# An attention and MLP kernel on one core: score slots handed over bank by bank, operands made earlier, fill products at the start, and a root by Ln and Exp

## The chip, the core and the metric

One Trainium2 chip, one of its cores. The metric is device microseconds from start to end of one execution; the median of three runs of the kernel before is 671.86 us (670.94 to 672.25). The core's engines run side by side, each in the order of its own program: TensorE (PE) for matrix products, VectorE (DVE) and GpSimd (POOL) for arithmetic on tiles, ScalarE (ACT) for functions and copies, and SyncE (SP), which issues most of the DMA transfers.

## The reference

Rotary attention over 4 batches, 8 heads, 576 positions and 64 channels per head; its result, as (batch, position, 512 channels), goes through a layer norm and a two-layer MLP with 2048 hidden channels and is added to it.

```
q_rot, k_rot = rotate(q), rotate(k)
scores = (q_rot @ k_rot^T) / sqrt(D)
attn = exp(scores - max(scores)); attn = attn / (sum(attn) + 1e-09)
x = concat over heads of attn @ v
mu, var = mean(x), mean((x - mu) ** 2)
xn = (x - mu) / sqrt(var + 1e-06) * g_ln
out = x + relu(xn @ w_ch1) @ w_ch2
```

All tensors are float32. The MLP's products are made of a high and a low part of each operand: three products (high weight by high and by low input, low weight by high input) stand for one.

## The kernel before

**Plan.** The kernel is first written down as tasks (`add`), each with an engine, the tasks it waits for and the buffers (`RINGS`, `LATE`) it takes and gives back. Two tables of digits, `PLACES` and `SIDES`, fix the order of the tasks and, for those that may run on DVE or on POOL, the engine. `Plan.run` goes through the tasks in that order and emits their instructions; every engine then works through its own in that order.

**Attention.** 16 pairs of heads, each in blocks of 128 queries. `scores` (L486, and L499 for the 64 queries left over) makes a block of scores in PSUM, in one of four "sc" banks of two halves; DVE finds the row maximum (L513), ACT the exponential with its sum (L520); transposes by identity products on PE (L580) or by DVE (L568) and copies (L598) follow; then pv (L654, L680) and the scaling into the row blocks xt (L692, L701, L706). Between these stand the decoding of the MLP's weights (L868 to L897) and, from the norm of block 0 on, that block's MLP in plain form (`mlp_unit`, L1007, its hidden values L1030 and L1034 and its sums L1044).

**Startup.** `warm` (L1310) multiplies the identity by itself 16 times on PE; `first_pair` loads keys, queries and the rotary table, and rotates them (L387): the first half of the keys, the query head (128 columns) and the second half of the keys on DVE, the remaining 448 queries on POOL. The memsets L361 to L364 stand between these.

**Layer norm.** For each of five row blocks: sums over channels (L759), mean by a product (L766), centring (L790), squares (L796), variance (L780), the root by ACT's Sqrt (L808) and DVE's reciprocal (L811), a spread of it over the partitions on PE (L816) and the scaling (L825). Block 0 goes to the plain MLP; blocks 1 to 4 are stored as "hats" (L838).

**Paired layers.** Blocks (1, 2) and then (3, 4), 448 columns each, go through the MLP in pairs with seven products in place of eight (`pair_stage`, L1180; the order of the products is 1, 6, 2, 7, 5, 4, 3). `pair_inputs` reloads the hats (L1126) and makes seven operands from differences of them (L1110), for two row groups: ACT rounds the high part (L1088), DVE or POOL makes the low part (L1095). A stage has two halves of six matmuls for each product; its PSUM slots "n", six halves, are read by DVE or ACT (L1221 to L1236 in a hidden stage, L1252 and L1276 in an output stage). The weights w come by DMA, 512 KB a product, some of them as sums made by L961 and L971. `switch` closes the attention's buffers and opens those of the paired layers, the "n" slots among them.

## Time and profile before

| | |
|---|---|
| median of 3 runs | 671.86 us (670.94 to 672.25) |
| profiled execution: its own time | 673.72 us |
| its span, from the first to the last instruction | 671.8 us |
| busy: PE, DVE, ACT, POOL | 630.5, 552.2, 358.5, 297.6 us |
| mean granted clock of PE | 0.987 of full speed |

The profile is of one execution. An engine's busy time is the time in which at least one of its instructions runs; idle time before an instruction is put down to what ended last before it began.

### The profile page before, as it was taken

The page shows a single profiled execution, that of the slowest core. Times are in us where ns is not written, and L with a number is a line of the kernel's source. Part 1 is how long each engine was busy: PE and PEld are TensorE (multiplying, and loading weights), DVE is VectorE, ACT ScalarE, POOL GpSimd, SP SyncE. Part 2 cuts the span into 40 slices and gives each one's busy share as a digit, 9 for nine tenths or more (in the row PEclk, how much of TensorE's full clock was granted, in tenths as well). Part 3 has the DMA queues.
Part 4 walks back from the last instruction along what each step waited for, and adds up shares of the span by engine and source line. Part 5 has one row for each costly group of instructions (what it writes and reads, how often), then busy time and mean ns, then how long its engine had stood idle before and what let it go on. Part 6 is the DMA issues. An engine that isn't in the chain of part 4 may idle for free.

```text
span 671.8 us, 13940 instructions
## 1 busy us (share of the span) xinstructions
PE 630.5 (94%) x5268; PEld 491.4 (73%) x5268; DVE 552.2 (82%) x887; ACT 358.5 (53%) x734; POOL 297.6 (44%) x223
## 2 busy tenths in 40 slices
PE   5899988999899999898898699899999999999997
PEld 4555647766675757666576587799889999999997
DVE  4998788589899989899955789978789786857876
ACT  2898877467678876688644246342343143223230
POOL 2636663454566558477510254853324212404042
PEclk7999998999999999999999899999999999999999
DMA  8477574668669889886877688778876887766666
GB/s 273 125 243 238 182 200 151 202 232 239 218 219 266 277 278 293 263 270 233 272 236 214 203 257 285 244 271 268 293 254 210 266 267 219 218 221 211 212 208 201
DMA packets 89283, 158.42 MB, mean 236 GB/s; under 512 B 11776, under 2 KB 57344, under 8 KB 88704
## 3 DMA queue, kind: packets, MB, share of 16 engines
q1 hardware_dynamic: 88080, 156.67, 73.2%
q10 hardware_dynamic: 1136, 0.85, 0.4%
q8 instruction: 42, 0.69, 0.4%
q14 instruction: 25, 0.20, 0.1%
HBM read 117.57 MB, written 39.92 MB: 234 GB/s over the span
## 4 chain that ended last, share of the span: by engine, by line
PE 64%; DVE 16%; DMA 8%; ACT 6%; issue 4%; POOL 1%; SPq 0%; ACTq 0%; DVEq 0%; POOLq 0%
PE n L1180 34%; PE sc L1007 9%; PE sc L486 6%; PE sc L654 5%; PE sc L680 4%; DVE mx L513 3%; PE sc L580 3%; ACT pt L520 2%; DMA w<-in_w2p 2%; DMA w<-s 2%; DVE pt L568 2%; DMA s<-ws 1%; ACT pt L598 1%; PE sc L499 1%; DVE tmp L1218 1%
## 5 line engine op out<-in xcount | busy, mean ns | idle before, releaser
L1180 PE MATMUL n<-x,w 128*128 128x448 f32 x672 | 143.0, 371 | 7.9 <-ACT x L1088 2.6
L1180 PEld LDWEIGHTS n<-x,w 128*128 128x128 f32 x672 | 126.5, 189 | 22.9 <-DVE x L1095 3.4
L520 ACT ACTIVATE pt<-sc,mx 128x576 f32<-128x576 f32 x144 | 105.7, 739 | 54.9 <-DVE mx L513 54.2
L1180 PE MATMUL n<-o,w 128*128 128x448 f32 x576 | 120.8, 368 | 1.9 <-DVE acc L1276 1.3
L513 DVE TENSOR_REDUCE mx<-sc 128x1 f32<-128x576 f32 x144 | 102.8, 747 | 19.5 <-PE sc L486 16.0
L1180 PEld LDWEIGHTS n<-o,w 128*128 128x128 f32 x576 | 107.7, 188 | 13.1 <-DVE acc L1276 1.7
L1088 ACT ACTIVATE o<-tmp 128x448 fp32r<-128x448 f32 x96 | 53.3, 574 | 103.1 <-PE n L1180 39.8
L486 PE MATMUL sc<-x 64*128 64x288 f32 x512 | 93.5, 442 | 8.4 <-DVE x L387 6.4
L486 PEld LDWEIGHTS sc<-x 64*128 64x128 f32 x512 | 53.1, 192 | 35.9 <-ACT pt L520 8.4
L1095 POOL TENSOR_TENSOR o<-tmp,o 128x448 fp32r<-128x448 f32 x33 | 43.1, 1319 | 81.8 <-ACT o L1088 71.5
L877 POOL TENSOR_TENSOR fw<-fw,w 128x512 int32<-128x512 int32 x32 | 43.3, 1356 | 55.7 <-ACT w L871 27.0
L1252 DVE TENSOR_TENSOR xt<-xt,n 128x448 f32<-128x448 f32 x80 | 47.8, 613 | 9.7 <-PE n L1180 8.5
L654 PE MATMUL sc<-pt,v 128*64 128x512 f32 (+2 forms) x324 | 50.5, 417 | 0.9 <-ACT pt L520 0.9
L680 PE MATMUL sc<-pt,v 32*64 32x160 f32 (+1 forms) x2016 | 43.7, 301 | 5.6 <-issue 2.1
L654 PEld LDWEIGHTS sc<-pt,v 128*64 128x64 f32 (+1 forms) x324 | 22.4, 142 | 33.7 <-issue 29.7
L680 PEld LDWEIGHTS sc<-pt,v 32*64 32x64 f32 x2016 | 36.7, 135 | 12.6 <-issue 6.6
L568 DVE STREAM_TRANSPOSE pt<-pt 128x1152 f32<-128x1152 f32 (+1 forms) x35 | 43.1, 1241 | 3.3 <-ACT pt L520 3.3
L1007 PE MATMUL sc<-xh,w 128*128 128x512 f32 x128 | 44.7, 410 | 0.7 <-ACT pt L520 0.7
L1007 PE MATMUL sc<-hh,w 128*128 128x512 f32 x128 | 44.3, 405 | 0.4 <-issue 0.4
L580 PE MATMUL sc<-ident,pt 128*128 128x128 f32 x288 | 38.1, 278 | 5.9 <-ACT pt L520 4.6
L1218 DVE SCALAR_TENSOR_TENSOR tmp<-tmp 128x448 f32<-128x448 f32 x48 | 40.6, 854 | 3.3 <-ACT tmp L1225 2.9
L580 PEld LDWEIGHTS sc<-ident,pt 128*128 128x128 f32 x288 | 31.3, 141 | 13.2 <-ACT pt L520 9.1
(129 smaller groups left out, 1062.2 us busy)
## 6 DMA issues: line engine op xcount, KB each, us to landing
w<-s SPq DMA_DIRECT2D x64, 512.0 KB
w<-v SPq DMA_DIRECT2D x96, 256.0 KB
s<-ws SPq DMA_DIRECT2D x24, 512.0 KB
v<-in_vp SPq DMA_DIRECT2D x37, 320.0 KB
x<-in_qk SPq DMA_DIRECT2D x30, 288.0 KB
xs<-in_qk SPq DMA_DIRECT2D x30, 288.0 KB
w<-in_w1p SPq DMA_DIRECT2D x16, 512.0 KB
w<-in_w2p SPq DMA_DIRECT2D x16, 512.0 KB
```

What stands on the lines that cost most here:

```text
L486: PE.matmul(ps[:, a, :HS], lhsT=q[r, c * P : (c + 1) * P], rhs=k[r, KEYS[a]], start=True, stop=True)
L513: DVE.tensor_reduce(out=mx, in_=st["ps", i, n][:, :, :HS], axis=AX.XY, op=ALU.max, negate=True)
L520: ACT.activation(out=halves(p), in_=st.pop(("ps", i, n))[:, :, :HS], func=AF.Exp, bias=st.pop(("mx", i, n)), scale=1.0, accum_out=total)
L568: DVE.transpose(p, p)
L580: PE.transpose(two[:, j, k * P : (k + 1) * P], p[:, at : at + P], ident)
L654: yield lambda o=o, x=x: PE.matmul(o, lhsT=w, rhs=x, start=start, stop=stop)
L680: PE.matmul(tiles[a // 2][j * D : (j + 1) * D, a % 2, x0 : x0 + (u1 - u0) * BLK], lhsT=v[r, of, k * P + j * D : k * P + (j + 1) * D], rhs= ...
L1007: PE.matmul(ps, lhsT=wt, rhs=x, start=c + m == 0, stop=c + m == NC + 1)
L1088: ACT.activation(out=o[0], in_=x(), func=AF.Relu if relu else AF.Copy)
L1180: PE.matmul(ps, lhsT=wt, rhs=x, start=fresh and kc + z == 0, stop=kc + z == 3, skip_group_check=True)
L1218: return lambda: DVE.scalar_tensor_tensor(out=out(), in0=x(), scalar=0.0, in1=y(), op0=ALU.max, op1=ALU.subtract)
L1252: DVE.tensor_tensor(out=o, in0=o, in1=ps(which, h), op=ALU.add)
```

## The change

Slots: the "n" slots are no longer a pool of their own. Three tasks, `pass0` to `pass2`, hand one "sc" bank each to the paired layers as the last tasks of attention that take a bank have started; one half of a bank is one slot. The bank for the norms of blocks 3 and 4 is whichever is left.

Startup: 20 warm products; five groups of five more (`FILLED`) behind score blocks 0, 0, 1, 1 and 2; the first loads are issued in the order rotary table, first keys, query head, second keys, other queries; the 448 other queries are rotated on DVE.

Root: ACT makes Ln and then Exp of -0.5 times it, from a table that has both and is loaded at the start; three DVE operations (one Newton step) follow in place of the reciprocal. The scores' Exp is from the same table.

Order: both tables are new (they are not shown), and with them the place of nearly every task. Among those that moved are the operands of the first paired stage, and product 1 of that stage, which now stands in the middle of the last pv.

```diff
-LATE = {"n": 6, "o": 13, "tmp": 9, "lf": 1, "ls": 1}
+LATE = {"o": 13, "tmp": 9, "lf": 1, "ls": 1}
...
-WARM = 16
+WARM = 20
+FILL, FILLED = 5, (0, 0, 1, 1, 2)
...
-            self.task, self.engine = t, e
-            self.trace(t.fn)
...
-    scp = passing("sc", space=PSUM)
-    kept = ctx.enter_context(tc.tile_pool(name="kept", bufs=1, space=PSUM, side="right"))
-    banks = [(kept if n == RINGS["sc"] - 1 else scp).tile([P, 2, 512], F32, name=f"sc{n}") for n in range(RINGS["sc"])]
+    scp = pool("sc", space=PSUM)
+    banks = [scp.tile([P, 2, 512], F32, name=f"sc{n}") for n in range(RINGS["sc"])]
...
+        ACT.preload_act_table_set("natural_log_exp_and_others")
...
-        l1 = dma(288, keys(KEYS[0]))
-        l2 = dma(128, queries(head))
+        l1 = dma(288, keys(KEYS[0]), behind=[l0])
+        l2 = dma(128, queries(head), behind=[l1])
         second.extend([(rope_sb[:, :, KEYS[1]], rope[:, :, KEYS[1]])] + keys(KEYS[1]))
         l3 = dma(288, [])
         l4 = dma(288, [])
-        l_q = dma(448, queries(rest))
+        l_q = dma(448, queries(rest), behind=[l2])
...
-        qq = rotate(xq, rest, [l3, l_q, k2], -70, "POOL", 1.15)
+        qq = rotate(xq, rest, [l3, l_q, k2], -70, "DVE", 0.64)
...
-            ACT.activation(out=z["std"], in_=z["var"][:, :Q], func=AF.Sqrt, bias=eps_ln, scale=1.0)
-
-        def inverse():
-            DVE.reciprocal(z["std"], z["std"])
+            ACT.activation(out=z["std"], in_=z["var"][:, :Q], func=AF.Ln, bias=eps_ln, scale=1.0)
+            ACT.activation(out=z["std"], in_=z["std"], func=AF.Exp, scale=-0.5)
+
+        def polish():
+            y = z["std"]
+            t = z["var"][:, :Q]
+            DVE.scalar_tensor_tensor(out=t, in0=t, scalar=1e-6, in1=y, op0=ALU.add, op1=ALU.mult)
+            DVE.scalar_tensor_tensor(out=t, in0=t, scalar=-0.5, in1=y, op0=ALU.mult, op1=ALU.mult)
+            DVE.scalar_tensor_tensor(out=y, in0=t, scalar=1.5, in1=y, op0=ALU.add, op1=ALU.mult)
 
         def spread():
             r = z["r"] = z["mu"]
             for k in range(4):
                 PE.matmul(r[:, k * Q : (k + 1) * Q], lhsT=quarter[:, k], rhs=z["std"], start=k == 0, stop=k == 3, skip_group_check=True)
 
-        t = add({"ACT": 1.7}, deviation, [v], N)
-        t = add({"DVE": 1.0}, inverse, [t], N)
+        t = add({"ACT": 0.75}, deviation, [v], N)
+        t = add({"DVE": 0.75}, polish, [t], N)
...
-                    bank[which, h] = late["n"].tile([P, 512], F32, name="n")
+                    bank[which, h] = late["n", plan.task.got["n"][0]]
...
+            if fresh:
+                at["n", which, h] = t
...
-            at["U", h] = add(evac, lambda: DVE.tensor_tensor(out=new("U"), in0=ps(1, h), in1=T("a"), op=ALU.add), [t, at["a", h]], -1.0, take=["tmp"], give=["tmp", "n"])
+            at["U", h] = add(evac, lambda: DVE.tensor_tensor(out=new("U"), in0=ps(1, h), in1=T("a"), op=ALU.add), [t, at["a", h]], -1.0, take=["tmp"], give=["tmp", "n"], of=at["n", which, h])
...
+    def warm(count):
+        ps = banks[plan.task.got["sc"][0]][:, 0].rearrange("p (k n) -> p k n", k=4)
+        for k in range(count):
             PE.matmul(ps[:, k % 4], lhsT=ident, rhs=ident, start=True, stop=True)
 
-    add({"PE": 0.8 + 0.31 * WARM}, warm, [c1], -97.0, take=["sc"], give=["sc"])
+    add({"PE": 0.8 + 0.31 * WARM}, lambda: warm(WARM), [c1], -97.0, take=["sc"], give=["sc"])
...
+    def keep_m():
+        late["m"] = banks[plan.task.got["sc"][0]]
+
+    add({"NONE": 0.0}, keep_m, attn, 0.0, take=["sc"], give=["m"])
...
+    for n, c in enumerate(FILLED):
+        t = add({"PE": 0.1 + 0.24 * FILL}, lambda: warm(FILL), [c1], -75.0 + n, behind=[ev["s", (0, c)]], take=["sc"], give=["sc"], name=f"fill{n}")
+        t.of = t
+        ev["late"].after.append(t)
+    held = add({"NONE": 0.0}, lambda: None, [], -100.0, take=["n"] * 6, name="held")
+    takers = [t for t in plan.tasks if "sc" in t.take]
+    last = []
+    for n in range(3):
+        def pass_on(n=n):
+            late["n", 2 * n], late["n", 2 * n + 1] = (banks[plan.task.got["sc"][0]][:, k] for k in range(2))
+
+        started = [t for t in takers if n == 2 or t.take.count("sc") > 1 or n == 1 and t in attn and not t.name.startswith("pv")]
+        last = [add({"NONE": 0.0}, pass_on, last, 0.0, take=["sc"], give=["n"] * 2, of=held, behind=started, name=f"pass{n}")]
```

On PE, the start of the program, before: warm products (L1310), then two blocks of scores (sc0 to sc3 are the banks).

```order
L1310 MATMUL sc0_108<-ident_200 128x128 x16
L486 MATMUL sc1_109<-x_208,x_210 128x288
L486 MATMUL sc2_110<-x_208,x_210 128x288
L486 MATMUL sc1_109<-x_208,x_210 128x288
L486 MATMUL sc2_110<-x_208,x_210 128x288
L486 MATMUL sc3_111<-x_208,x_210 128x288
L486 MATMUL sc0_108<-x_208,x_210 128x288
L486 MATMUL sc3_111<-x_208,x_210 128x288
```

The same place after (L1319 warm and fill, L489 scores).

```order
L1319 MATMUL sc0_105<-ident_197 128x128 x20
L489 MATMUL sc1_106<-x_205,x_207 128x288
L489 MATMUL sc2_107<-x_205,x_207 128x288
L1319 MATMUL sc3_108<-ident_197 128x128 x5
L489 MATMUL sc1_106<-x_205,x_207 128x288
L489 MATMUL sc2_107<-x_205,x_207 128x288
L1319 MATMUL sc0_105<-ident_197 128x128 x5
L489 MATMUL sc3_108<-x_205,x_207 128x288
L489 MATMUL sc0_105<-x_205,x_207 128x288
L489 MATMUL sc3_108<-x_205,x_207 128x288
L489 MATMUL sc0_105<-x_205,x_207 128x288
L1319 MATMUL sc1_106<-ident_197 128x128 x5
```

Groups of five identity products now stand behind the first half of a block's scores, behind the second, and so on.

On ACT, the norm of block 0 in the middle of attention, before: L808 is the root, L520 the exponential of scores, and each has its load of a table.

```order
L796 ACTIVATE sq_1101<-xc_1082 128x512
L796 ACTIVATE sq_1110<-xc_1082 128x512
L796 ACTIVATE sq_1119<-xc_1082 128x512
L520 ACTIVATE pt_1084,total1_207<-sc1_109,mx_1104 128x576
L520 ACTIVATE pt_1084,total1_207<-sc2_110,mx_1112 128x576
L808 ACT_TABLE_LOAD
L808 ACTIVATE std_1133<-sc3_111,eps_ln_203 128x128
L868 ACTIVATE fw_885<-w64_1062 128x512
```

The same place after: L811 is Ln, L812 Exp, L523 the exponential of scores.

```order
L523 ACTIVATE pt_1110,total1_204<-sc1_106,mx_1136 128x576
L799 ACTIVATE sq_1146<-xc_1107 128x512
L523 ACTIVATE pt_1110,total1_204<-sc0_105,mx_1144 128x576
L799 ACTIVATE sq_1164<-xc_1107 128x512
L601 COPY pt_1110<-sc1_106 128x2x512
L811 ACTIVATE std_1172<-sc2_107,eps_ln_200 128x128
L812 ACTIVATE std_1172<-std_1172 128x128
```

Both table loads are gone, and Exp of the root stands right behind its Ln.

On DVE, the operands of the first paired stage, before (x01 is product 1's operand of row group 0; L1095 a low part, L1110 a difference): they stand behind the last scalings of attention (L701, L706).

```order
L1095 TENSOR_TENSOR x01_4377<-xc_3931,x01_4377 128x448
L1110 TENSOR_TENSOR xc_3931<-xc_3931 128x448
L1095 TENSOR_TENSOR x11_4379<-sq_3933,x11_4379 128x448
L1095 TENSOR_TENSOR x13_4385<-sq_3975,x13_4385 128x448
L1110 TENSOR_TENSOR sq_3933<-sq_3963,sq_3933 128x448
L1110 TENSOR_TENSOR sq_3963<-sq_3975,sq_3963 128x448
L1095 TENSOR_TENSOR x03_4382<-xc_3931,x03_4382 128x448
L1110 TENSOR_TENSOR xc_3931<-xc_3931 128x448
L1110 TENSOR_TENSOR sq_3975<-sq_3975,sq_3933 128x448
L1110 TENSOR_TENSOR xc_3931<-xc_3931 128x448
```

After, most of these are on POOL, behind the last weights of attention and ahead of its sums of weights (L969).

```order
L1117 TENSOR_TENSOR sq_3917<-sq_4109,sq_3917 128x448
L1102 TENSOR_TENSOR x01_4185<-xc_3913,x01_4185 128x448
L1117 TENSOR_TENSOR xc_3913<-xc_3913 128x448
L1102 TENSOR_TENSOR x13_4225<-sq_4152,x13_4225 128x448
L1102 TENSOR_TENSOR x03_4192<-xc_3913,x03_4192 128x448
L1117 TENSOR_TENSOR xc_3913<-xc_3913 128x448
L1117 TENSOR_TENSOR sq_4109<-sq_4152,sq_4109 128x448
L1117 TENSOR_TENSOR xc_3913<-xc_3913 128x448 x2
L1102 TENSOR_TENSOR x16_4365<-sq_4152,x16_4365 128x448
L1102 TENSOR_TENSOR x17_4264<-sq_4109,x17_4264 128x448
L1117 TENSOR_TENSOR acc_4211<-acc_4211,sq_4152 128x448
L1102 TENSOR_TENSOR x05_4368<-xc_3913,x05_4368 128x448
```

Four of the rest are on DVE ahead of the last scalings of attention (L704, L709); L1102 is the low part here.

```order
L1052 TENSOR_TENSOR xt0_632<-xt0_632,sc2_107 128x512
L1117 TENSOR_TENSOR sq_4152<-sq_4152,sq_3917 128x448
L1102 TENSOR_TENSOR x12_4320<-acc_4211,x12_4320 128x448
L1102 TENSOR_TENSOR x06_4354<-xc_3913,x06_4354 128x448
L1102 TENSOR_TENSOR x02_4322<-xc_3913,x02_4322 128x448
L1102 TENSOR_TENSOR x15_4356<-sq_3917,x15_4356 128x448
L704 TENSOR_TENSOR xt3_2708<-sc0_105,inv_4348 128x64
L704 TENSOR_TENSOR xt3_2708<-sc3_108,inv_4348 128x64
```

So the low parts and differences moved to another engine, and those that stayed moved ahead of the scalings.

On DVE, the evacuations of the first paired stage, before, with what each waits for; an n tile is one slot.

```order
L1230 TENSOR_TENSOR tmp_4559<-n_4549,tmp_4559 128x448 [waits PE_49]
L1233 TENSOR_TENSOR tmp_4587<-n_4509,tmp_4507 128x448 [waits PE_49]
L1233 TENSOR_TENSOR tmp_4595<-n_4523,tmp_4545 128x448 [waits PE_49]
L1093 SCALAR_TENSOR_TENSOR o_4593<-tmp_4547,o_4593 128x448 [waits Activation_49]
L1236 TENSOR_TENSOR tmp_4507<-n_4534,tmp_4507 128x448 [waits DVE_49,PE_49]
L790 TENSOR_TENSOR xc_4620<-xt3_2662,sc3_111 128x448
L1236 TENSOR_TENSOR tmp_4545<-n_4549,tmp_4545 128x448 [waits DVE_49,PE_49]
```

After; sc2 and sc3 are banks, and each is read twice, once for each half.

```order
L1237 TENSOR_TENSOR tmp_4572<-sc3_108,tmp_4519 128x448 [waits DVE_49,PE_49]
L1237 TENSOR_TENSOR tmp_4578<-sc3_108,tmp_4526 128x448 [waits DVE_49]
L1239 TENSOR_TENSOR tmp_4572<-sc2_107,tmp_4572 128x448 [waits DVE_49,PE_49]
L1239 TENSOR_TENSOR tmp_4578<-sc2_107,tmp_4578 128x448 [waits DVE_49]
L1100 SCALAR_TENSOR_TENSOR o_4600<-tmp_4578,o_4600 128x448 [waits Activation_49]
L1242 TENSOR_TENSOR tmp_4613<-sc3_108,tmp_4519 128x448 [waits PE_49]
L1242 TENSOR_TENSOR tmp_4624<-sc3_108,tmp_4526 128x448
L1245 TENSOR_TENSOR tmp_4526<-sc2_107,tmp_4526 128x448 [waits DVE_49,PE_49]
L1245 TENSOR_TENSOR tmp_4519<-sc2_107,tmp_4519 128x448
```

Where each reader waited for PE by itself, now the first of two does, and the second has no wait for PE.

## Rows read from the trace of the kernel before

**Rows 1.** The page, part 1: busy time, share of the span, instructions.

```profile
PE 630.5 (94%) x5268; PEld 491.4 (73%) x5268; DVE 552.2 (82%) x887; ACT 358.5 (53%) x734; POOL 297.6 (44%) x223
```

**Rows 2.** The page, part 4: the chain that ended last, by engine.

```profile
PE 64%; DVE 16%; DMA 8%; ACT 6%; issue 4%; POOL 1%; SPq 0%; ACTq 0%; DVEq 0%; POOLq 0%
```

**Rows 3.** PE by stretch: us, length, busy (records), clock, DMA share, GB/s.

```profile
0.00:10.00 10.00, 6.01 (x32) 0.97 0.77 234
10.00:20.00 10.00, 6.21 (x23) 0.52 0.73 258
19.00:20.00 1.00, 1.00 (x6) 0.70 0.00 0
20.00:30.00 10.00, 7.46 (x52) 1.00 0.34 107
96.00:108.00 12.00, 8.45 (x74) 1.00 0.92 267
108.00:112.00 4.00, 3.89 (x132) 0.57 0.02 4
300.00:320.00 20.00, 17.65 (x362) 1.00 0.72 225
355.00:366.00 11.00, 9.19 (x50) 1.00 0.98 255
373.40:385.00 11.60, 6.64 (x27) 0.85 0.76 255
402.00:445.00 43.00, 39.42 (x196) 1.00 0.79 266
500.00:650.00 150.00, 150.00 (x732) 1.00 0.72 225
```

**Rows 4.** Startup, timelines of PE and DVE: start, duration, instruction, idle before.

```profile
5.79 1.58 PE L1310 MATMUL sc<-ident 128*128 128x128 f32 x12
13.79 3.25 PE L486 MATMUL sc<-x 64*128 64x288 f32 x12 [6.42 <-DVE x L387]
6.96 0.46 DVE L387 TENSOR_TENSOR xs<-xs,rope_sb 128x288 f32<-128x288 f32 x1 [5.87 <-DMA x<-in_qk]
...
7.84 0.48 DVE L361 MEMSET quarter<- 128x512 f32 x1
8.41 0.85 DVE L363 MEMSET quarter<- 1x128 f32 x4
...
10.44 1.21 DVE L387 TENSOR_TENSOR xs<-xs,rope_sb 128x128 f32<-128x128 f32 x1
11.57 0.28 DVE L387 TENSOR_TENSOR x<-x,rope_sb 128x128 f32<-128x128 f32 x1
```

**Rows 5.** ACT's timeline at the norm of block 0.

```profile
102.80 1.28 ACT L808 ACT_TABLE_LOAD   x1
...
105.93 1.28 ACT L520 ACT_TABLE_LOAD   x1
107.23 0.74 ACT L520 ACTIVATE pt<-sc,mx 128x576 f32<-128x576 f32 x1
```

**Rows 6.** The root and reciprocal: ns minimum, median, maximum, first and last start.

```profile
L808 ACT ACTIVATE std<-sc,eps_ln x5: 350/354/367, 104.1 to 456.7; 128x112 f32<-128x112 f32 x4, 128x128 f32<-128x128 f32 x1
L811 DVE RECIPROCAL std<-std x5: 836/852/952, 104.5 to 457.1; 128x112 f32<-128x112 f32 x4, 128x128 f32<-128x128 f32 x1
```

**Rows 7.** PE's waits from 372 to 384 us: total, times, longest.

```profile
PE n L1180 <- ACT x L1088: 2.6, 1, 2.6
PE n L1180 <- DVE x L1095: 2.4, 3, 1.6
```

**Rows 8.** Timelines around the transition, and low parts on either engine.

```profile
371.71 0.69 DVE L1044 TENSOR_TENSOR xt<-xt,sc 128x512 f32<-128x512 f32 x1 [5.79 <-PE sc L1007]
382.59 3.85 POOL L961 TENSOR_TENSOR lf<-lf 128x512 f32<-128x512 f32 x1 [32.40 <-DMA lf<-f]
L1095 DVE TENSOR_TENSOR x<-xc,x x13: 606/616/785, 374.8 to 531.7; 128x448 fp32r<-128x448 f32 x13
L1095 POOL TENSOR_TENSOR x<-sq,x x3: 1152/1185/1539, 483.9 to 512.4; 128x448 fp32r<-128x448 f32 x3
```

More of the change, by code (lines that the diff above doesn't have):

```diff
@@ L250, in run @@
             self.length = max(self.length, t.end)
+            self.task, self.engine = t, e
+            self.trace(t.fn)
             for r in t.give:
@@ L373, in first_pair, with dma @@
         head, rest = slice(0, P), slice(P, S)
-        def dma(kb, pairs, prio=-90.0):
+        def dma(kb, pairs, prio=-90.0, behind=()):
             def go():
@@ L378, in go @@
                     SP.dma_start(o, i)
[L380 removed]
+            if not pairs:
+                return add({"NONE": 6.2}, go, (), prio)
+            return add({"SP": kb / RATE + (1.8 if prio < -90 else 0.0)}, go, (), prio, parts=(len(pairs), 0.45), behind=behind)
         def rotate(x, r, loads, prio, e, dur):
@@ L763, in mean @@
         def mean():
-            two = banks[RINGS["sc"] - 1 if ring == "m" else plan.task.got["sc"][0]]
+            two = late["m"] if ring == "m" else banks[plan.task.got["sc"][0]]
             z["mu"], z["var"] = two[:, 0], two[:, 1]
@@ L1222, in hidden @@
         elif i == 6:
-            at["U", h] = add(evac, lambda: DVE.tensor_tensor(out=new("U"), in0=ps(1, h), in1=T("a"), op=ALU.add), [t, at["a", h]], -1.0, take=["tmp"], give=["tmp", "n"])
+            at["U", h] = add(evac, lambda: DVE.tensor_tensor(out=new("U"), in0=ps(1, h), in1=T("a"), op=ALU.add), [t, at["a", h]], -1.0, take=["tmp"], give=["tmp", "n"], of=at["n", which, h])
         elif i == 2:
-            r = at["r", h] = add({"ACT": ROUND}, lambda: ACT.activation(out=new("r"), in_=ps(0, h), func=AF.Relu), [t], -1.0, take=["tmp"], give=["n"])
+            r = at["r", h] = add({"ACT": ROUND}, lambda: ACT.activation(out=new("r"), in_=ps(0, h), func=AF.Relu), [t], -1.0, take=["tmp"], give=["n"], of=at["n", which, h])
             at["l1", h] = operand(key(1), lambda: T("r"), [r], -0.5, "h")
@@ L1232, in hidden @@
         elif i == 4:
-            c21 = at["c21", h] = add(evac, lambda: DVE.tensor_tensor(out=new("c"), in0=ps(2, h), in1=T("U"), op=ALU.add), [t, at["U", h]], -1.0, take=["tmp"], give=["n"])
+            c21 = at["c21", h] = add(evac, lambda: DVE.tensor_tensor(out=new("c"), in0=ps(2, h), in1=T("U"), op=ALU.add), [t, at["U", h]], -1.0, take=["tmp"], give=["n"], of=at["n", which, h])
             at["l2", h] = operand(key(2), lambda: T("c"), [c21], -0.5, ring_of(3), relu=True)
         elif i == 3:
-            c12 = add(evac, lambda: DVE.tensor_tensor(out=T("U"), in0=ps(3, h), in1=T("U"), op=ALU.add), [t, at["c21", h]], -1.0, give=["n"])
+            c12 = add(evac, lambda: DVE.tensor_tensor(out=T("U"), in0=ps(3, h), in1=T("U"), op=ALU.add), [t, at["c21", h]], -1.0, give=["n"], of=at["n", which, h])
             t1 = add(evac, fold(lambda: T("U"), lambda: T("U"), lambda: T("r")), [c12, at["r", h]], -0.5, port=True)
@@ L1252, in go @@
                 DVE.tensor_tensor(out=o, in0=o, in1=ps(which, h), op=ALU.add)
-            at["read", which, h] = add(evac, go, [t] + list(after), -1.0, give=give)
+            at["read", which, h] = add(evac, go, [t] + list(after), -1.0, give=give, of=at["n", which, h])
             ev["xo", n, c] = at["read", which, h]
@@ L1279, in outputs @@
             how = {"ACT": ROUND} if g == 0 and i == 1 else evac
-            at["read", which, h] = ev["acc", q, h] = add(how, total, [t] + ([ev["acc", q, h]] if ("acc", q, h) in ev else []), -1.0, give=["n"] if i == 6 else [])
+            at["read", which, h] = ev["acc", q, h] = add(how, total, [t] + ([ev["acc", q, h]] if ("acc", q, h) in ev else []), -1.0, give=["n"] if i == 6 else [], of=at["n", which, h])
             if i == 6 and g == 3:
@@ L1330, in rope_attention_then_ln_mlp @@
             weight_sums(k // NC % 2, k // (2 * NC))
-    add({"NONE": 0.0}, lambda: None, attn, 0.0, take=["sc"], which=RINGS["sc"] - 1, give=["m"])
     work = [t for t in plan.tasks if t not in attn]
+    def keep_m():
+        late["m"] = banks[plan.task.got["sc"][0]]
+    add({"NONE": 0.0}, keep_m, attn, 0.0, take=["sc"], give=["m"])
     for k in range(PAIR0):
```

125 lines of the change are left out of this document (60 added, 65 removed).

## The prediction, made before the changed kernel was run

> **What bounds the kernel now.** I read the busy line first: TensorE (PE) works 630.5 of the 671.8 us span, 94%; no other engine is over 82% [rows 1]. The chain that ended last confirms it: 64% is PE, 16% DVE, 8% DMA, 6% ACT [rows 2]. So time comes only from PE's waits (671.8 - 630.5 = 41.3 us in all), from stretches in which PE runs at half clock, and from PE work that is added or removed. The table by stretch says where these are [rows 3]. At the start, 0 to 30 us, PE is busy 6.01 + 6.21 + 7.46 us, and the clock of the middle ten is 0.52. From 96 to 108 us, where the layer norm of block 0 stands in the middle of attention, PE is busy 8.45 of 12; the four microseconds behind it run at 0.57. From 300 to 320, the norm of block 2, it is busy 17.65 of 20. From 355 to 366 and from 373.4 to 385, where attention ends and the paired layers begin, 9.19 of 11 and 6.64 of 11.6, the second at a mean clock of 0.85. From 402 to 445, 39.42 of 43. Between 500 and 650 PE is busy all of 150 us, with 732 matmuls: 0.205 us each, and nothing to win but by less work.
>
> [...]
>
> **Startup.** The first score waits 6.42 us for DVE and comes at 13.79 [rows 4]. DVE has its first operands at 6.96; the new order puts in front of that score three operations on the query head (0.28 each, the row at 11.57), three on the first keys (0.46 each, the row at 6.96) and the memsets (0.48, 0.85 and a small one): 3.6 us. Before, an operation on the second keys stood ahead of it too, and one on the head took 1.21 us. If the query head lands with the keys the first score comes at 6.96 + 3.6 = 10.6; if only when DVE first read it before (10.44), at 14.0. I take 11.0, 2.8 us earlier, since its load is issued right behind two others. Against this stand 4 more warm products and 25 fill products. The 16 of before are the 32 records of 6.01 us [rows 3], 0.376 us each; the four lie in a wait, the 25 are 9.4 us of new PE work. Budget from 10 to 30 us: 13.67 us of work as before, less 3.0 if the clock stays up, plus 9.4, is 20.1 us; from 11.0 that ends at 31.1, against 30. But DVE and ACT begin as much earlier as PE does, and before they were what PE waited for. Sum zero, between -2.5 (everything shifts with the first score) and +2.5 (the fills all lie on the path, and the clock gives back nothing in half of the stretch).
>
> **The root of the norm.** ACT loads the table of the square root at 102.80 (1.28 us) and that of the exponential at 105.93 (1.28), and the scores' exponential, on which the next transposes wait, comes at 107.23 [rows 5]. With Ln and Exp from one table both loads go: 7 loads over the program, 9.0 us of ACT. [...] The extra Exp is about 0.35 us, as the root itself. [...] PE's wait for this step stays. What makes it cheaper is the order: PE has pv products to do while the norm's chain runs. PE idles 3.55 us there and loses 1.7 to the clock behind it; I take -3.0 of these 5.3 (bounds -1.5, only what the loads held up beside other waits, and -5). At the norm of block 2, PE idle 2.35 with the same pair of loads: -1.5 (0 to -2.3). The other three norms: -0.5 (0 to -1).
>
> **The transition.** PE's waits from 373.4 on are for operands of the first paired products: 2.6 us for a rounding on ACT, 2.4 for lows on DVE [rows 7]. Yet DVE stood idle 5.79 us just before, and POOL 32.40 us up to 382.6 [rows 8]: the operands were late because they came late in the order. Now 16 of the 22 differences and lows are POOL's and stand before its sums of weights; six stay on DVE, ahead of the last scalings. One POOL operation of this kind is about 1.19 us with the neighbour quiet and up to 1.54 [rows 8], so the chain lasts 19 to 25 us. PE's work between the last scores (360.5) and product 1 is 24 matmuls of about 0.23 and half of pv, some 8 us; product 6, which needs the ninth of the chain, follows 5 us later. Started when POOL fell idle and the hats had landed, by about 358, the ninth ends at 369 (or 372 at 1.54), product 6 is due at about 373. That is enough, barely. PE idles 1.81 + 4.96 us in the two windows and loses 1.0 to the clock: 7.8 us. I take -6.5 (bounds -3.5, if half the operands still come after their product, and -8). Most of DVE's operand work behind 373.4, at 0.62 an operation, goes from there too, and with them the late evacuations of the next stages: of the 3.58 us of idle from 402 to 445 I take -1.5 (0 to -3.5).
>
> **Slots.** A bank with two halves takes the place of separate slots. In the changed program's order a reader of the first half often waits for the matmuls into the second half too: six at 0.205, 1.2 us later, and the reader of the second has no wait of its own. PE goes on meanwhile in another bank, and there are three; DVE is 82% busy, so it is often later than that anyway. +0.5, between 0 and +3.
>
> Sum: 0 - 3.0 - 1.5 - 0.5 - 6.5 - 1.5 + 0.5 = -12.5. The profiled execution took 673.72, 1.86 above the median of 671.86; -12.5 on the median gives **659.4 us**.
>
> **Rivals.** *The wait moves to POOL (0.20).* DVE's product beside a busy POOL took 1.21 where a quiet one of the same shape took 0.28 [rows 4], and the POOL operations spread from 1.15 to 1.54. If both slow each other while DVE does the last scores' maxima and transposes, the chain is 25 us or more, the transition saves 2 instead of 6.5, and the stages behind it nothing: 659.4 + 4.5 + 1.5 = 665.4. The same comes out if the hats land late. [...]
>
> *The fills don't hold the clock (0.10).* In the trace the warm products end at 7.37 [rows 4], PE waits, the ten us from 10 run at 0.52, and the clock is back only in the microsecond from 19 (0.70) [rows 3]. After, PE still waits from 7.37 + 4 x 0.376 = 8.9 to 11.0. If it falls there, three fills run at the low level, at up to 0.75 us a product: 5.6 us more and no 3.0 given back, 20.1 + 3.0 + 5.6 from 11.0 is 39.7 in place of 30, less what DVE's pace covers; I take +6, 665.4.
>
> *Slower: the bank halves (0.12).* Paired layers have 220 evacuations of a half bank. In the new program some 80 of them more than before wait for the other half's six matmuls. Each is worth 1.2 us if PE then lacks a free bank or an operand, so all would be near 100 us; the change is lost once 10 or 11 are on the path (12.5 / 1.2). Against it: PE waits for nothing from 500 to 650 us, so there is slack, and three banks of two products each are 7.4 us deep. It would give 672 and more, I take 676.
>
> **How the numbers follow.** The forecast has 0.58, with a range of its own of 654 to 665. The range 652 to 669 adds the two rivals at 665 and the better bounds; it leaves out the slower case and a few hundredths at the lower end. A measurement of this kernel can tell about 0.2% (1.3 us) from no change. Faster by more than that: 0.58 + 0.18 + 0.07 = 0.83; same: 0.06; slower: 0.11, nearly all the bank halves.
>
> **What would show it.** First score near 11 us and clock 1.0 from 10 to 20, with PE's position at 30 us within 2.5 us of before. One table load instead of 8, and PE busy above 10.5 of the 12 us around the first norm, with no stretch at the low clock behind it. Between the last scores and the third paired product PE idle under 2 us, and POOL busy through it. In the paired layers, waits of PE for DVE under 3 us in all, and 0.205 us a matmul as before. I am wrong if PE waits on POOL's lows at product 6 or 2, if the clock is low until 20 us, or if long waits for an evacuation stand in the stretch that had none.

## The result and the profile after

| | before | changed |
|---|---|---|
| median of the runs (lowest to highest) | 671.40 us (668.53 to 672.25, 4 runs) | 678.01 us (677.54 to 680.99, 4 runs) |
| profiled execution, span | 673.72, 671.8 us | 678.40, 676.5 us |

The ratio is 1.0109, with a 95% interval of 1.0076 to 1.0141: slower by 1.1%, where 1.9% faster was forecast. The busy line of the page after, against [rows 1]:

```profile
PE 636.2 (94%) x5326; PEld 494.3 (73%) x5326; DVE 542.0 (80%) x881; ACT 351.8 (52%) x732; POOL 313.4 (46%) x239
```

PE's idle time is 676.5 - 636.2 = 40.3 us, where it was 41.3: as much as before, in other places. PE by stretch after, against [rows 3]; the columns are the same:

```profile
0.00:10.00 10.00, 6.78 (x40) 1.00 0.81 259
10.00:20.00 10.00, 9.28 (x69) 1.00 0.69 249
20.00:30.00 10.00, 9.04 (x70) 1.00 0.40 137
96.00:108.00 12.00, 10.34 (x215) 1.00 0.76 227
108.00:112.00 4.00, 3.94 (x152) 1.00 0.19 53
260.00:300.00 40.00, 36.70 (x466) 0.96 0.70 242
300.00:320.00 20.00, 16.63 (x357) 1.00 0.92 269
320.00:355.00 35.00, 30.59 (x442) 0.95 0.57 174
355.00:366.00 11.00, 9.22 (x53) 0.91 0.90 224
373.40:385.00 11.60, 10.78 (x213) 1.00 0.92 275
402.00:445.00 43.00, 41.51 (x209) 1.00 0.85 282
500.00:650.00 150.00, 146.43 (x704) 1.00 0.71 218
```

Two stretches that [rows 3] does not have, in the kernel before:

```profile
260.00:300.00 40.00, 38.22 (x485) 1.00 0.87 277
320.00:355.00 35.00, 33.57 (x458) 1.00 0.80 254
```

The start, the norm of block 0, the first paired products and the stretch from 402 to 445 are better, as forecast: idle 3.55 us becomes 1.66 at the norm, 4.96 becomes 0.82 from 373.4, 3.58 becomes 1.49 from 402, and both stretches of low clock of [rows 3] that lay at the start and behind the norm are at 1.00. But from 260 to 366 there are new idle times (3.30 us in place of 1.78 up to 300, 4.41 in place of 1.43 from 320 to 355) and a new low clock, and the 150 us that PE filled with 732 paired matmuls hold 704 now. The loss lies in places that the prediction took for safe.

The place of PE's work shows it in one view. The table gives the start, in us, of the n-th record of a kind on PE, counted through the whole timeline (inside a row of several records the start is interpolated, which makes it uncertain by some 0.4 us). A score is a matmul of a block of scores, a paired record a matmul of the paired layers. The third and fourth columns are experiments of the next section, after_pad36 and hp_again.

```
record                      before  changed  +half a piece  +half a piece, separate halves
score 0                       13.8     10.7       10.8          10.5
score 40                      28.8     26.7       27.2          26.7
plain MLP 95                 145.2    141.1      140.8         141.7
score 440                    255.7    248.6      250.7         249.1
score 480                    283.3    282.2      277.4         277.0
score 600                    342.3    343.6      333.5         333.2
pv 2015 (last)               373.5    380.8      365.7         365.8
paired 84                    398.5    396.6      381.0         381.7
paired 504                   495.7    491.9      479.6         473.7
paired 1008                  599.4    601.4      589.8         580.0
paired 1343 (last)           668.2    672.9      661.2         649.2
```

The changed kernel is 7 us ahead at 249 us, 6 of these are gone at score 480, and from paired 504 on it loses 8.5 more.

**The first loss: pauses inside pv.** PE's timeline after in the pv stretches, and the row of the page on PE's queue of instructions:

```profile
268.74 2.43 PE L683 MATMUL sc<-pt,v 32*64 32x160 f32 x128 [0.35 <-issue]
274.11 0.43 PE L683 MATMUL sc<-pt,v 32*64 32x160 f32 x2 [2.95 <-issue]
317.08 2.41 PE L683 MATMUL sc<-pt,v 32*64 32x128 f32 x121 [1.61 <-issue]
342.27 0.65 PE L683 MATMUL sc<-pt,v 32*64 32x160 f32 x19 [3.63 <-issue]
```

```profile
q8 instruction: 42, 0.69, 0.4%
```

A product here is a small matmul of pv. "Issue" means that PE waited for nothing that the profile shows. Between two of the pauses lie exactly 128 products, and each product is a weight load and a matmul: 256 instructions. The row of the queue gives 42 packets for 0.69 MB, 16.4 KB each; counted from the built program PE has 10,800 instructions, so a packet is 257 of them. I numbered PE's instructions through the program (two a record, one a wait): all four pauses start at number 193 or 194 of a piece of 256, counted from the program's first instruction, so a border lies there. So do, in the traces of all eleven experiments below, the kernel before and this one, 47 of the 48 pauses of 0.25 us or more that are put down to issue ahead of 390 us. PE ran through a piece that is pv alone in 2.43 us, and the next piece had not come: from the start of such a piece to the start of the next it took 5.37 us at 268.74 and 6.1 at 336.2. The trace also has the packets of this queue one by one, and they settle it: each of the 47 pauses ends 1.2 to 1.6 us behind the end of one. The packet that the pause up to 274.11 waited for ran from 271.73 to 272.61, the one for 342.27 from 339.95 to 340.94.

The pauses of 2.95 and 3.63 us are followed by the low clock: a granted clock of 0.50 from 275.3 to 278.7 and from 343.6 to 347.0 us.

**The second loss: waits in the paired layers.** PE's waits from 500 to 650 us after, where before there were none [rows 3]:

```profile
PE sc L1187 <- DVE xt L1261: 2.2, 3, 0.9
PE sc L1187 <- DVE acc L1285: 0.7, 1, 0.7
```

One of them, in the timelines of DVE and of PE:

```profile
504.68 0.62 DVE L1285 TENSOR_TENSOR acc<-acc,sc 128x448 f32<-128x448 f32 x1 [1.34 <-PE sc L1187]
505.36 6.82 PE L1187 MATMUL sc<-o,w 128*128 128x448 f32 x30 [0.71 <-DVE acc L1285]
```

DVE stands for 1.34 us for PE, and then PE stands for DVE. An evacuation is the reading of a slot out of PSUM. The semaphore value for which that evacuation waits belongs to a matmul 36 later than the last one into its own half; its own had started 8.9 us before. In the built program 58 of the 103 evacuations on DVE with a wait for PE wait like this for matmuls into the other half of the bank; in the kernel before none of 143. On ACT it is 15 of 23, and none of 33 before. Of the 58, 36 wait for six matmuls more than they need, the other 22 for 12 to 174.

The waits listed come to less than the loss. A paired matmul starts 0.205 us behind the one before it, but its record lasts 0.37, so a delay of up to 0.16 us leaves no idle time in the profile. The 704 matmuls at 0.205 are 144.3 us: 5.7 of the 150 us are lost, 3.57 of them as idle time.

### The profile page after: what moved, and what is told of

Its sections match the earlier page's. It is cut to its first block, busy times and chain, and to the rows that moved or that the text cites. A ratio compares the mean times of both kernels' runs of the same rounds, so it can differ in the third digit from the quotient of the medians.

```text
span 676.5 us, 14036 instructions
## 1 busy us (share of the span) xinstructions
PE 636.2 (94%) x5326; PEld 494.3 (73%) x5326; DVE 542.0 (80%) x881; ACT 351.8 (52%) x732; POOL 313.4 (46%) x239
## 4 chain that ended last, share of the span: by engine, by line
PE 71%; DVE 13%; DMA 5%; ACT 4%; issue 4%; SPq 1%; POOL 1%; DVEq 0%; POOLq 0%; ACTq 0%
PE sc L1187 36%; PE sc L1015 10%; PE sc L489 8%; PE sc L683 5%; PE sc L657 4%; PE sc L583 4%; DVE mx L516 3%; DVE xt L1261 2%; ACT pt L523 2%; DMA x<-in_qk 1%; DVE pt L571 1%; DMA s<-ws 1%; DMA v<-in_vp 1%; DMA w<-in_w2p 1%; DVE tmp L1227 1%
## 5 line engine op out<-in xcount | busy, mean ns | idle before, releaser
L1187 PE MATMUL sc<-x,w 128*128 128x448 f32 x672 | 141.6, 369 | 3.3 <-issue 1.0
L1187 PEld LDWEIGHTS sc<-x,w 128*128 128x128 f32 x672 | 125.2, 188 | 18.4 <-ACT tmp L1230 1.6
L523 ACT ACTIVATE pt<-sc,mx 128x576 f32<-128x576 f32 x144 | 105.8, 739 | 59.7 <-DVE mx L516 57.8
L1187 PE MATMUL sc<-o,w 128*128 128x448 f32 x576 | 123.8, 370 | 5.9 <-DVE xt L1261 3.5
L1187 PEld LDWEIGHTS sc<-o,w 128*128 128x128 f32 x576 | 106.6, 188 | 20.9 <-DVE xt L1261 6.6
L1095 ACT ACTIVATE o<-tmp 128x448 fp32r<-128x448 f32 x96 | 53.3, 576 | 113.7 <-DVE tmp L1227 52.7
L489 PE MATMUL sc<-x 64*128 64x288 f32 x512 | 88.2, 433 | 7.5 <-DVE x L390 2.6
L489 PEld LDWEIGHTS sc<-x 64*128 64x128 f32 x512 | 50.1, 188 | 32.3 <-ACT pt L523 6.3
L1102 POOL TENSOR_TENSOR o<-tmp,o 128x448 fp32r<-128x448 f32 x31 | 38.2, 1244 | 64.8 <-ACT o L1095 64.7
L1261 DVE TENSOR_TENSOR xt<-xt,sc 128x448 f32<-128x448 f32 x80 | 47.2, 617 | 11.9 <-PE sc L1187 11.1
L683 PE MATMUL sc<-pt,v 32*64 32x160 f32 (+1 forms) x2016 | 43.8, 300 | 10.1 <-issue 9.4
L601 ACT COPY pt<-sc 128x1024 f32<-128x1024 f32 x36 | 36.2, 1016 | 8.3 <-PE sc L583 8.1
```

What stands on the lines that cost most here:

```text
L489: PE.matmul(ps[:, a, :HS], lhsT=q[r, c * P : (c + 1) * P], rhs=k[r, KEYS[a]], start=True, stop=True)
L523: ACT.activation(out=halves(p), in_=st.pop(("ps", i, n))[:, :, :HS], func=AF.Exp, bias=st.pop(("mx", i, n)), scale=1.0, accum_out=total)
L683: PE.matmul(tiles[a // 2][j * D : (j + 1) * D, a % 2, x0 : x0 + (u1 - u0) * BLK], lhsT=v[r, of, k * P + j * D : k * P + (j + 1) * D], rhs= ...
L1095: ACT.activation(out=o[0], in_=x(), func=AF.Relu if relu else AF.Copy)
L1187: PE.matmul(ps, lhsT=wt, rhs=x, start=fresh and kc + z == 0, stop=kc + z == 3, skip_group_check=True)
L1261: DVE.tensor_tensor(out=o, in0=o, in1=ps(which, h), op=ALU.add)
```

## The experiments

All medians are of runs beside the kernel before on the same chip. The changed kernel's own 678.01 was measured in another session, beside 671.40; where a difference to it is given below, the ratios make it some 5% smaller (1.0109 to 0.9988 is 8.1 us where the medians give 8.6, 1.0109 to 0.9879 is 15.4 where they give 16.1).

| label | median us (lowest to highest, runs) | before | ratio, 95% |
|---|---|---|---|
| after_pad36 | 669.37 (666.01 to 672.60, 10) | 670.33 | 0.9988, 0.9956 to 1.0020 |
| before_pad32 | 676.25 (673.09 to 679.52, 4) | 670.33 | 1.0106, 1.0043 to 1.0170 |
| after_halves | 661.87 (659.55 to 665.42, 4) | 670.33 | 0.9879, 0.9823 to 0.9935 |
| after_halves_pad | 656.91 (652.33 to 661.11, 4) | 670.33 | 0.9815, 0.9744 to 0.9887 |
| hp_again | 654.74 (651.45 to 657.66, 6) | 668.82 | 0.9785, 0.9749 to 0.9822 |
| halves_pad64 | 664.47 (660.35 to 665.74, 7) | 668.82 | 0.9923, 0.9895 to 0.9952 |
| hp_sqrt | 656.24 (654.20 to 658.00, 6) | 668.82 | 0.9806, 0.9777 to 0.9835 |
| hp_smallfill | 653.63 (652.06 to 655.07, 6) | 668.82 | 0.9769, 0.9741 to 0.9798 |
| before_pad64 | 670.39 (666.47 to 673.37, 12) | 669.10 | 1.0017, 0.9990 to 1.0044 |
| before_lnexp | 667.90 (664.61 to 673.66, 12) | 669.10 | 0.9980, 0.9952 to 1.0009 |
| hp_dve_operands | 656.22 (652.77 to 659.48, 6) | 669.10 | 0.9816, 0.9781 to 0.9850 |

**Half a piece of instructions in the changed kernel (after_pad36).** The edit, in `warm`:

```diff
-        for k in range(count):
-            PE.matmul(ps[:, k % 4], lhsT=ident, rhs=ident, start=True, stop=True)
+        for k in range(count + (36 if count == WARM else 0)):
+            PE.matmul(ps[:, k % 4] if k < count else ps[:32, k % 4, :32], lhsT=ident if k < count else ident[:, :32], rhs=ident if k < count else ident[:, :32], start=True, stop=True)
```

> The changed kernel with 36 small products (128x32 by 32 columns, 72 records, 144 of PE's instructions) behind the warm products; their results are never read, all else is the same. They lie in PE's wait for the first score. Theory A (PE's program arrives in pieces of 256 instructions, and PE stands still where it runs through a piece faster than the next arrives): in the changed kernel the three pauses put down to issue (2.95, 1.61 and 3.63 us, in the three pv stretches at 268 to 342 us) all begin at the same position within a piece, and two of the pieces are nothing but pv products. The shift by 144 puts the borders elsewhere, no piece of pv alone is left, the 2.95 and 3.63 go below 1.5 together, and the low clock behind each goes: 6 to 10 us less, about 669 to 672 us. Rival (the pauses come from the load on the transfers at that moment, or from another engine that the profile does not name): the pauses stay at the same place in the program, 678 us.

It came to 669.37, 8.6 us less. The pauses of 0.25 us or more that are left are two (PE's timeline):

```profile
312.22 1.43 PE L683 MATMUL sc<-pt,v 32*64 32x160 f32 x65 [0.82 <-issue]
...
329.41 3.51 PE L683 MATMUL sc<-pt,v 32*64 32x128 f32 x192
333.98 0.76 PE L683 MATMUL sc<-pt,v 32*64 32x128 f32 x21
335.35 1.59 PE L683 MATMUL sc<-pt,v 32*64 32x128 f32 x75 [0.61 <-issue]
```

The 192 products that held the pause of 3.63 us run through. In the table of places PE is 4.8 us ahead of the changed kernel at score 480, 10.1 at score 600 and 15.1 at the last pv; some 4 are given back in the paired layers. Over the trace up to 390 us the pauses at borders come to 1.4 us, where the changed kernel has 9.8. Work that nobody reads, 36 products of it, made the kernel as fast as the one before.

**Half a piece in the kernel before (before_pad32)**, the same edit with 32 products behind the 16 of L1310.

> The kernel before with 32 such small products (128 instructions) behind its warm products. Theory A: of its pieces now some are nothing but pv products (one at about 267 us, one at about 365), which none was; pauses of 2 to 4 us appear there, 3 to 8 us more with the clock, about 675 to 679. The products fall in the wait of 6.4 us before the first score and could keep the clock up, which would give back up to 3 us at the start; so what decides is whether new pauses of PE, put down to issue, stand at those pv stretches. Rival: no new pauses, 668 to 672.

1.1% slower, though the small products lie in a wait of 6.4 us. In its timeline of PE:

```profile
271.05 0.80 PE L680 MATMUL sc<-pt,v 32*64 32x160 f32 x31 [1.59 <-issue]
...
371.06 1.19 PE L680 MATMUL sc<-pt,v 32*64 32x160 f32 x56 [1.58 <-issue]
```

Pauses in pv of 4.2 us in all against 2.1, each at number 193 of a piece: new pauses came where theory A puts them, though they are shorter than the 2 to 4 us expected. They account for some 2 of the 5.9 us. The rest is open: the execution traced, 673.09 us, is the fastest of the four, and no slower than the one traced of the kernel before.

**A whole piece (before_pad64, halves_pad64)**: 64 small products, 256 instructions, which leave every border where it was.

> The kernel before with 64 small products behind its warm products, 256 of PE's instructions and so a whole piece: the borders lie where they lay without them. Theory A: the pauses put down to issue are those of the kernel before (2.1 us at pv stretches, none over 1.6), and the time is the kernel before's within 3 us, where half a piece (32 products) made it 1.1% slower. Rival (small products at the start cost by themselves): as slow as with 32, about 674 to 677.

> Separate halves, and 64 small products behind the warm ones in place of 36: 256 of PE's instructions, a whole piece, so that every border of a piece lies where it lay without them. Theory A: the gain of the 36 is gone, pauses put down to issue stand at the pv stretches near 272, 315 and 320, 340 and 371 us as in the kernel with separate halves alone, about 6 us in all, and the time is 4 to 6 us above the kernel with 36 (660 to 664; 0.5 of it from the products themselves, which end some 0.5 us behind the point at which the first score could start). Rival (the small products help by themselves, through the clock or the start): 655 to 658 again.

In the kernel before a whole piece changes nothing that can be told (1.0017). In the changed order with separate halves it gives 664.47 where half a piece gave 654.74 beside it: 9.7 us for 28 small products more. Of these some 1.9 are the products themselves, which hold the first score back from 10.53 to 12.40 us, where 0.5 was expected. The pauses are back, 9.2 us of them against 1.3; PE's timeline:

```profile
271.17 2.43 PE L683 MATMUL sc<-pt,v 32*64 32x160 f32 x128 [0.59 <-issue]
276.81 0.69 PE L683 MATMUL sc<-pt,v 32*64 32x160 f32 x2 [3.22 <-issue]
```

So it is not the small products that help, it is where the borders fall. Half a piece against none, with separate halves, is worth less: 5.0 us by the medians of after_halves and after_halves_pad below, four runs each, with pauses of 9.2 and 2.4 us.

**Separate halves (after_halves).** Each bank has a pool of its own, which is closed when the bank is handed over, and two tiles are opened in its place; the order of every engine stays. In the built program no evacuation on DVE waits for the other half any more (0 of 130).

```diff
-    scp = pool("sc", space=PSUM)
-    banks = [scp.tile([P, 2, 512], F32, name=f"sc{n}") for n in range(RINGS["sc"])]
+    banked = {n: ctx.enter_context(ExitStack()) for n in (0, 3, 2, 1)}
+    banks = {n: e.enter_context(tc.tile_pool(name=f"sc{n}", bufs=1, space=PSUM, side="right" if n == 1 else "left")).tile([P, 2, 512], F32, name=f"sc{n}") for n, e in banked.items()}
...
-            late["n", 2 * n], late["n", 2 * n + 1] = (banks[plan.task.got["sc"][0]][:, k] for k in range(2))
+            banked[plan.task.got["sc"][0]].close(); slots = ctx.enter_context(tc.tile_pool(name=f"late_n{n}", bufs=1, space=PSUM, side="right", reuse_waits="tile")); late.update({("n", 2 * n + k): slots.tile([P, 512], F32, name=f"n{2 * n + k}") for k in range(2)})
```

> The changed kernel with each bank in a pool of its own, closed when it is handed over, and its two halves opened again as two tiles, one a slot. The order of every engine stays the same; in the built program the evacuations of paired products that wait for matmuls of another slot go from 58 of 103 (with a wait for PE, on DVE) to 0 of 130. Theory B (readers of a half that wait for the other half cost PE its waits for DVE in the paired layers): PE's idle time from 445 to 650, 5.7 us in the changed kernel, goes below 2.5, and PE's place from 490 us on no longer falls behind that of the kernel before; 4 to 8 us less, about 670 to 674. Rival (the order of DVE's work in the paired layers is late by itself): at most 1 us less, and the waits of PE for evacuations stay.

661.87, 16.1 us less than the changed kernel: twice what I expected. PE from 500 to 650 us, and its only wait for DVE there:

```profile
500.00:650.00 150.00, 149.66 (x728) 1.00 0.72 224
```

```profile
PE n L1187 <- DVE xt L1261: 0.2, 1, 0.2
```

**Both (after_halves_pad, and again as hp_again).**

> Both edits at once. If A and B are the two causes and do not overlap: 10 to 18 us less than the changed kernel, 660 to 668, faster than the kernel before. If one of them is not a cause: 668 to 674. If neither: 678.

> The kernel with separate halves and 36 small products once more, as the measure for the three that are run beside it on the same chip. Both theories: 655 to 659 us.

656.91 and 654.74: 1.9% and 2.2% faster than the kernel before, and a little below the 660 to 668 and the 655 to 659 expected. The two cures together are worth 21.1 us (678.01 to 656.91), less than the sum of the 8.6 and 16.1 that each gave alone; the intervals are too wide to say whether they win in part the same time. PE by stretch in hp_again:

```profile
260.00:300.00 40.00, 39.51 (x493) 1.00 0.84 272
320.00:355.00 35.00, 33.95 (x472) 1.00 0.68 214
355.00:366.00 11.00, 11.00 (x313) 1.00 0.90 258
...
500.00:650.00 150.00, 148.37 (x722) 1.00 0.73 224
```

The last two columns of the table of places set the halves apart from everything else: the same to within 2 us up to paired 84, then 5.9 us apart at paired 504, 9.8 at 1008 and 12.0 at the end. In this pair of traces two slots in one tile cost nothing in attention, and 12 us over the paired layers. Two traces of one kernel can differ by half as much (after_halves_pad is 6.5 us behind hp_again at paired 504), but the other traces agree on the place. From paired 84 to paired 1343 PE takes 276.1 and 280.1 us in the two kernels with two slots in one tile, 263.7 to 269.8 in the seven with separate halves, and 264.3 to 269.3 in the four with the kernel before's own slots.

**The root undone (hp_sqrt), and alone (before_lnexp).** The first puts Sqrt and the reciprocal back into the version with both cures; the second puts the new root, and the line that loads its table, into the kernel before.

> Separate halves and 36 small products, but the root made as before the change, by ACT's Sqrt and DVE's reciprocal: seven loads of ACT's table come back, PE's program is the same. Prediction's step (the root is worth 2 to 4 us, at the norms of blocks 0 and 2, where ACT's load stands ahead of exponentials that PE waits for): 2 to 4 us slower, 659 to 661. Rival (in this order PE has pv products to do while the norm's chain runs, so the loads cost nothing): within 1 us.

> The kernel before with the new root alone (Ln, Exp and three operations on DVE, one table for all of it): seven loads of ACT's table fewer, the order and PE's program the same. The prediction's step takes 2 to 4 us for what the loads hold up at the norms of blocks 0 and 2; from the reverse edit in the changed order, which cost 1.5, I now expect 1 to 3 us faster than the kernel before, 666 to 668. Rival: the waits of PE there are for DVE's own steps (the centring and the root), and nothing changes.

1.5 us slower and 1.2 us faster, below the 2 to 4 us that the prediction's step takes; neither can be told from no change. The medians put the root at 1 to 1.5 us in either order; that it is above zero is likely and not shown.

**Small fills (hp_smallfill)**: the 25 fill products made as small as the padding, `k < count == WARM` in place of `k < count` in the edit above.

> Separate halves and 36 small products, and the 25 fill products replaced by as many small ones (128x32 by 32 columns): the same number of instructions, some 6 us less of PE's work between 11 and 25 us. Prediction's step (fills and clock cancel): within 1.5 us. If the fills are what holds the clock, it falls to the low level between 11 and 20 us and the scores there take twice as long; ACT and DVE, which set the pace behind 25 us, then begin up to 2 us later: up to 2 us slower. If they only cost, up to 3 us faster.

653.63 against 654.74, no difference that can be told, and the clock (in the timeline by stretch of PE) does not need them:

```profile
11.00:12.00 1.00, 1.00 (x15) 1.00 1.03 392
12.00:14.00 2.00, 1.76 (x23) 1.00 1.04 400
14.00:16.00 2.00, 1.25 (x18) 1.00 0.93 310
```

**The operands on DVE (hp_dve_operands)**: the low parts and differences of the first paired stage that stand on POOL are issued on DVE instead, at their places in the order.

```diff
-                eng().tensor_tensor(out=lo, in0=x(), in1=raw(hi), op=ALU.subtract)
+                (DVE if key[:2] == (0, 0) else eng()).tensor_tensor(out=lo, in0=x(), in1=raw(hi), op=ALU.subtract)
...
-            return lambda: eng().tensor_tensor(out=o(), in0=u(), in1=v(), op=ALU.subtract)
+            return lambda: (eng() if q else DVE).tensor_tensor(out=o(), in0=u(), in1=v(), op=ALU.subtract)
```

> Separate halves and 36 small products, and the 16 operands of the first paired stage that the change gave to POOL put on DVE, at the places in the order that they have. Prediction's step (POOL's idle time takes them, and DVE could not in time): some 9 us more of DVE's work stand between the last maxima and the scalings, PE waits again for operands or for exponentials behind late maxima, 3 to 6 us slower, 658 to 661. Rival (only the earlier place matters; DVE has 5.8 us of idle time there as well): within 1.5 us of the kernel with POOL, 653 to 656.

656.22, a ratio of 0.9816 against 0.9785 with POOL, with intervals that overlap: the rival, to 0.2 us. The engine makes no difference that can be told here. That the earlier place in the order is what counted follows only if the operands made the gain at all; no run put them back to their old place.

The reverse of the halves, the kernel before with two slots in one tile, was not run.

## Why the prediction was wrong

**The step that failed is "Slots": +0.5, between 0 and +3.** It measured 16.1 us without the padding (678.01 to 661.87) and 12.5 with it (669.37 to 656.91). The mechanism stood there and again among the rivals, with 1.2 us an evacuation and some 80 of them, but the sum took it at almost nothing and the rival at a chance of 0.12. That the rival's price of 676 is 2 us from the result is in part luck: with the pauses at borders gone the slots alone leave 669.4. Two arguments for the small price were wrong. "PE goes on in another bank, and there are three": PE takes its matmuls in their order, and the one at 505.36 stood 0.71 us until its slot had been read, whichever other bank was free. And "PE waits for nothing from 500 to 650, so there is slack": that PE never waited in that order showed that readers were in time there, not by how much; it was not a row about slack at all. Nor was the wait always six matmuls: at 504.68 it was 36. The count of readers was near, some 80 forecast and 73 found.

**A second cost was missing: where the order puts the borders of the instruction pieces.** The sum has no term for it. It measured 8.6 us (678.01 to 669.37) in the changed kernel, and with separate halves 5.0 (661.87 to 656.91), or 7.8 of the 9.7 against a whole piece (664.47 to 654.74) when the later first score is taken off. Its trace was there: two pauses put down to issue in the pv stretches of the kernel before, of which the prediction says nothing, begin at numbers 194 and 193 of a piece.

```profile
175.98 1.30 PE L680 MATMUL sc<-pt,v 32*64 32x128 f32 x52 [1.54 <-issue]
274.21 1.58 PE L680 MATMUL sc<-pt,v 32*64 32x128 f32 x71 [0.51 <-issue]
```

**The 3.0, 1.7 and 1.0 us that the steps take for the low clock are estimates.** Each is PE's busy time in [rows 3] times what the mean clock lacks of 1.00: 6.21 x 0.48, 3.89 x 0.43, 6.64 x 0.15. No run shows such a loss as a time of its own. What the traces show is a granted clock of 0.50 in the kernel before, from 9.4 to 19.6, from 108.3 to 111.8 and from 381.4 to 384.8 us, and of 1.00 in all three stretches in the changed one; and the pace of PE: 12 scores in 3.25 us before [rows 4], eight in 1.24 us after (from 14.71), and 184 products of pv in 5.16 us before (from 108.11), 121 in 2.41 us after (from 317.08).

The rest of the sum, 13 us without "Slots", came out as a total: with both costs gone the new order is 13.4 and 14.1 us faster than the kernel before. That the total is so near is in part luck, since some of its steps came out larger and some smaller. The steps below are read from single traces; hp_again's is 19.0 us shorter than that of the kernel before where the medians are 14.1 apart, so they can be too large by a few us together. By its steps:

- **Startup, 0 (-2.5 to +2.5):** the first score starts at 10.72 (11.0 forecast), the clock stays at 1.00, and score 40 is 2.1 us ahead. The fills were over-priced: ten records take 1.38 us, so a product is about 0.26, not the 0.376 of the warm products.

```profile
10.72 0.76 PE L489 MATMUL sc<-x 64*128 64x288 f32 x4 [2.58 <-DVE x L390]
11.40 1.38 PE L1319 MATMUL sc<-ident 128*128 128x128 f32 x10
```

- **The rival of the clock** did not come; but the full fills are not needed for it, since it stayed up with small ones too. What was still different from before is the wait ahead of the first score, 2.58 us in the changed kernel and below 0.3 in the run with small fills, in place of 6.42.
- **The root and the norm of block 0, -3.0:** plain MLP 95 is 4.1 us ahead where score 40 was 2.1, so -2. ACT's timeline, against [rows 5], has no load:

```profile
103.73 0.38 ACT L811 ACTIVATE std<-sc,eps_ln 128x128 f32<-128x128 f32 x1
104.14 0.31 ACT L812 ACTIVATE std<-std 128x128 f32<-128x128 f32 x1
104.77 0.74 ACT L523 ACTIVATE pt<-sc,mx 128x576 f32<-128x576 f32 x1 [0.32 <-DVE mx L516]
```

 The three new operations on DVE took 0.27 to 0.30 us each, one input in PSUM included, in place of a reciprocal of 0.85 [rows 6]. By the medians of the two experiments on the root 1.2 to 1.5 us over the whole program is the loads' (by the interval of before_lnexp at most 3.2); that the rest is the order, which gives PE pv to do, is what remains and not a run of its own. The same step at block 2 (-1.5) did not come: from 300 to 320 PE is idle 3.37 us where it was 2.35, 1.61 of it a pause at a border; without that, 1.76, some 0.6 less than before.
- **The transition, -6.5:** with both costs gone PE gains 9.0 us up to the last score and 16.8 up to paired 84 (hp_again against before: 351.4 to 360.4, then 381.7 to 398.5), so -7.8. All traces agree that this is the large gain: from the last score to paired 84 PE takes 38.5 to 42.1 us in the four traces in the order of before, and 29.2 to 31.6 in the six with the new order and half a piece. The changed kernel itself takes 34.7: pauses and a wait of 1.78 us for an exponential at 364, with the low clock (0.50 from 364.1 to 367.4) behind it, hid about half.
- **The wait moves to POOL (rival, 0.20):** it did not. POOL's chain started at 360.48 and not at 358, and stood 4.63 us for ACT's roundings. The operand of product 6 is also the tenth of the chain and not the ninth, so it came 9 us later than I had it; but its operations took 1.13 to 1.31 us, near the quiet price, and product 6 stood at 380.74, 8 us later than I had it. That both came late by about as much is luck.

```profile
360.48 1.13 POOL L1117 TENSOR_TENSOR sq<-sq 128x448 f32<-128x448 f32 x1 [17.82 <-DVE x L1102]
...
375.50 1.31 POOL L1117 TENSOR_TENSOR xc<-xc 128x448 f32<-128x448 f32 x1 [4.63 <-ACT x L1095]
376.78 2.23 POOL L1102 TENSOR_TENSOR x<-sq,x 128x448 fp32r<-128x448 f32 x2
```

 The startup rows behind this rival are less clean than I read them. DVE's product of 0.28 us at 11.57 had POOL's next one beside it for nearly all of its length (POOL's timeline, before):

```profile
11.58 1.27 POOL L387 TENSOR_TENSOR x<-x,xs 128x448 f32<-128x448 f32 x1
```

- **First paired stages, -1.5:** idle from 402 to 445 fell by 2.1 in the changed kernel. A gain over the paired layers as a whole is not shown: 263.7 to 269.8 us from paired 84 on with separate halves, 264.3 to 269.3 before.

What stays open: why a piece took 2.7 us to come at one border and 6.1 at another. The transfer is not what differs: the packets took 1.06 and 0.98 us, and PE went on 1.33 us behind each. They began 0.3 and 3.8 us behind the start of the piece before, and why the second began so late is not shown. The longest lie in stretches with a DMA share of 0.9 and more, but the 6.1 us at 336.2 reach into a quiet one. And 4 of the 15 us that the padding gains up to paired 84 in after_pad36 are lost again in the paired layers; no run was made on that.

## What to carry to other kernels

Two buffers in one tile were one buffer for 58 of the 103 evacuations on DVE that wait for PE here: before handing halves out as slots, count in the program as built for which write each reader waits. An engine that never waits in one order (PE, busy 150.00 of 150 us before) says nothing of the slack in another (146.43 of 150 after); look for the reader's lateness, not for the writer's idle time. And a long run of small instructions (here 128 products in 2.43 us) has to be laid against the borders of the program's pieces: pauses put down to issue, at a fixed distance in instructions, are a row to read, and moving the program by half a piece is a cheap test (8.6 us here), with a whole piece as its control.

## What the runs showed that I had not expected

PE's program came in pieces of 256 instructions (42 packets for 10,800), and 128 small products in a row (2.43 us) outran them: pauses of up to 3.63 us, each ending 1.2 to 1.6 us behind the end of a packet of the queue of instructions, and the low clock (0.50) behind the longest. 144 instructions whose results nobody reads, laid at the start of the program, were worth 8.6 us of 678. In hp_smallfill the clock stayed at 1.00 through stretches from 12 to 16 us in which PE was busy 1.76 and 1.25 of 2.
